# Second layer's weights decoded from copies shifted by 16 bits, and sums of low parts from the fourth tile on

## Chip, cores and metric

The kernel runs on one core of one Trainium2 chip. The metric is device time in microseconds of one execution, median of three runs. TensorE (PE), VectorE (DVE), ScalarE (ACT), GpSimd (POOL) and SyncE (SP) each work through their own queue in order and meet at semaphores.

## What is computed

A causal depthwise convolution over the sequence (7 softmaxed taps per head) is followed by two feed-forward layers without bias, all in float32 precision:

```python
out = einsum('hk,bskhg->bshg', softmax(weight), windows(x))   # x: (4, 4096, 192)
x = out.reshape(16384, 192)
h = x @ moe_w_in;  r = maximum(h, 0);  x = (r * r) @ moe_w_out       # 192 -> 2048 -> 192
h = x @ moe2_w_in; g = maximum(0.01 * h, h); out = g @ moe2_w_out
```

The four weight matrices arrive as float64 and are seen by the kernel as pairs of 32-bit words (low word, high word).

## The kernel before

**Precision.** PE multiplies in a float32 format with a shortened mantissa (`F32R`). Every operand is therefore split into a high part and a low part, and a product is made of high by high, high by low and low by high.

**Tiles and steps.** The 16384 tokens are 32 tiles of 512. A step is one pair p (0 to 7) of 128-wide chunks of the 2048 hidden columns, for one tile and one layer. Steps 0 to 15 take tiles 0 and 1 of layer 1 together; steps 16 to 23 are tile 2 of layer 1, 24 to 31 tile 3 of layer 1, 32 to 39 tile 0 of layer 2, and so on, 512 in all. In step s PE does the first product (`g1`) of step s+1, and the second product (`g2` or `g2_one`) of step s-2 (`LAG = 2`). PE works in two halves of 64 rows side by side, so that matmuls come in pairs; `g1` has 9 pairs. `g2_one` has 10 pairs as long as the low parts of the two chunks are multiplied apart, and 9 once a third operand, the sum of both low parts (`add_low`, tile `both`, written by DVE), and differences of weight blocks (`differences`, on POOL) let one product stand for two. Which of the two is used is `trick = s >= THREE`, with `THREE = 32`.

**What ACT and DVE do in a step.** ACT takes both chunks out of PSUM (`act`), squares them in layer 1 (`square`) and rounds them to the high part (`high`); DVE subtracts to get the low part (`low`), and adds where `trick` holds (`add_low`). The convolution of later tiles (`prep`), the splitting of results for the next layer (`leave`) and the decoding of weights (`dec`) are fitted between these by a planner (`fill` in `single`) with modelled costs; in steps 0 to 15 the order is written out by hand (`ROW`, one letter an operation: `L` a load of weights, `d` the next item of `dec`).

**Turns on a PSUM bank.** The two halves of PE take turns on the same accumulating bank. Where a bank goes from one half to the other, the order is kept by an empty instruction on POOL's queue that PE waits for:

```python
if holder.get((u, k), half) != half:
    done = nc.gpsimd.nop(nofuse=True).ins
    tc.add_manual_dep(done, lastly[u, k].name, in_turn, reason="halves take turns on a bank")
    tc.add_manual_dep(ins, done.name, in_turn, reason="halves take turns on a bank")
```

There is one of these in each paired step (L670) and three in each single step (L718). Nothing else on POOL is busy for long; its queue also issues a few DMAs (casts and integer adds) and runs `differences`.

**Decoding a weight.** The weights of one pair p of one layer are 768 pairs of words on each of 128 partitions, loaded by five DMAs on SP (`load`, `load_w`). For layer 2 DVE does: `mantissa` (L234) and `rest` (L250), which make the bits under the float32 mantissa from the low word; `exponent` (L266), after which ACT corrects the exponent (L269); `sign` (L281), followed by four DMAs on SP that put the high part in its places (L287); `power` (L296) and `low_` (L302, three pieces). Layer-2 pairs are decoded one after the other in about steps 13 to 38. The raw words of a pair lie in the memory that later holds the finished weights of another pair of layer 2 (`lent`, tags `w20` to `w27`), or in the staging tiles `y` and `w`.

Of the kernel before, what the change touches and what calls it, by code (L numbers as in the profile page):

```python
# [9 lines left out]
F32 = mybir.dt.float32  # L10
F32R = mybir.dt.float32r
I32 = mybir.dt.int32
U32 = mybir.dt.uint32
ACTF = mybir.ActivationFunctionType
ALU = mybir.AluOpType
# [3 lines left out]
P = 128  # L19
TT = 512  # L20
# [5 lines left out]
LAG = 2  # L26
AHEAD = 2
GAP = 5
SECOND, THIRD = 16, 36
THREE = 32  # L30
COVER = 2
# [7 lines left out]
CAST = ((1, 2), (1, 3))  # L39
ASIDE = (2, 3, 4)  # L40

# [13 lines left out]
    "ybpdwLAyBdpawThrp",  # L55
    "ldppABabhlp",
    "AyBydpabhdww",
    "lyAdappLhlBdwp",
    "pAbpayhBrbywd",
# [7 lines left out]
def conv_moe_moe2_kernel(  # L67
# [10 lines left out]
    nc = tc.nc  # L78
# [82 lines left out]
    def load_w(l, p, t):  # L161
# [10 lines left out]
        nc.sync.dma_start(out=to[:, :, 0:2 * R], in_=src[:, :, 2 * P:])  # L172

    held, holding = deque(), [False]
    ready, owner_m, raised_at, signed = {}, {}, {}, {}
# [24 lines left out]
    def decode(l, p, t, a, b):  # L200
# [22 lines left out]
        T = {}  # L223
        by_add = l == 1 and p >= ADD

        def mantissa():
# [27 lines left out]
        def exponent():  # L254
            release()
            if l == 1 and p > 0:
                if "t" not in words:
                    words["t"] = lent(0)
                T["t"] = words["t"][:, p % 2 * NW:(p % 2 + 1) * NW]
            elif l == 2 and p in ASIDE:  # L260
                if "t2" not in words:
                    words["t2"] = stage.tile([P, NW, 2], I32, tag="y", name="t2").rearrange("p n w -> p (n w)")
                T["t"] = words["t2"][:, p % 2 * NW:(p % 2 + 1) * NW]
# [28 lines left out]
        def power():  # L292
            if not (l == 1 and p > 0):
                owner_m["m"] = 0
            T["p"] = stage.tile([P, NW], I32, tag="t" if l == 1 and p > 0 else "m", name="p")[:, 0:n]
            nc.vector.tensor_scalar(out=T["p"], in0=T["t"], scalar1=-(2 ** 23), scalar2=None, op0=ALU.bitwise_and)  # L296

        def low_():
            assert not by_add or "added" in T
            ready[l, p, 1] = True  # L300
            for of, to in lows:
                nc.vector.scalar_tensor_tensor(  # L302
                    out=to, in0=of(T["r"]) if by_add else f32(of(lo_w)), scalar=2.0 ** -20, in1=f32(of(T["p"])), op0=ALU.mult, op1=ALU.mult
                )

        return [(one, mantissa), (two, rest)], [(one, exponent)], [(two, sign), (one, power), (two, low_)]


# [532 lines left out]
    def evac(u):  # L841
# [11 lines left out]
        def shift(i):  # L853
            if i == 0:
                z["s"], z["r"] = f32(stage.tile([P, NW], I32, tag="m", name="zs")[:, 0:TT]), ring[:, 2, :]
            nc.scalar.copy(out=z["s"][halves(i)], in_=o[i, "r"][halves(1 - i)])
# [27 lines left out]
    with tc.manual_schedule():  # L884
# [7 lines left out]
        def load(n):  # L892
# [3 lines left out]
            since[n] = now[0]  # L896
            if n < NP or NP + 1 < n < 2 * NP - 1:
                t = lent(n if n < NP else n + 1 - NP).rearrange("p (c w) -> p c w", w=2)
            else:
                t = stage.tile([P, NW, 2], I32, tag="w" if n == NP + 1 else "y", name="w")  # L900
            load_w(l, p, t)
            words[n] = t

        def fill_dec():
# [8 lines left out]
            def stage_(j, k):  # L913
                if j >= len(parts):
                    return
                n, a, b = parts[j]
                cost = {0: (780, 1180), 1: (620,), 2: (1230, 580, 1260)}
                l, p = loads[n]
                need = first_use["w", l, p] - LEAD_W - (((2 if p >= ADD else 3), 1, 0) if l == 1 else (4, 2, 1))[k]
                for m, c in enumerate(cost[k]):  # L920
                    def run(j=j, k=k, m=m, n=n):
                        if j not in got:
                            begin(j)
                        got[j][k][m][1]()
                    run.second = (k, m) in ((0, 1), (2, 2))
# [3 lines left out]
                    if l == 2 and k == 1 and p:  # L929
                        at_ = p - 2 if p in ASIDE[1:] else ASIDE[0] - 1 if p == ASIDE[-1] + 1 else p - 1  # L930
                        gate = lambda at_=at_: (p == ASIDE[0] or signed[2, at_] + 5000 <= clock["D"]) and not (
                            SECOND <= now[0] < THIRD and now[0] % NP == NP - 1
                        )
                    dec.append((need + (LATE and l == 1 and p >= ADD and (k, m) == (2, 2)) + (l == 2 and k == 2 and m > 0), c, run, gate))
                if k == 2 and a == 0:
                    if n in AFTER:
                        dec.append((need, 0, lambda n=n: load(AFTER[n]), None))

            stage_(0, 1)
            stage_(0, 0)  # L940
            for j in range(len(parts)):
                if parts[j][0] == NP - 1 or j == 0:
                    stage_(j, 2)
                    stage_(j + 1, 0)
                    stage_(j + 1, 1)
                else:
                    stage_(j + 1, 0)
                    early = j + 1 < len(parts) and parts[j + 1][0] - NP in ASIDE + (ASIDE[-1] + 1,)
                    if early:
                        stage_(j + 1, 1)  # L950
                    stage_(j, 2)
                    if not early:
                        stage_(j + 1, 1)
            for k in range(len(dec) - 2, -1, -1):
# [224 lines left out]
        def single(s, begun, u2, A, Z, leaving, then, alone):  # L1179
# [26 lines left out]
            do = {  # L1206
                "actA": lambda: act(*A), "actZ": lambda: act(*Z), "sqZ": lambda: square(*Z, trick), "sqA": lambda: square(*A, False),
                "hiA": lambda: high(*A), "hiZ": lambda: high(*Z), "loA": lambda: low(*A), "loZ": lambda: low(*Z),
# [33 lines left out]
        for s in range(NS):  # L1242
# [63 lines left out]
            begun += length(s - 1)  # L1306
            if s == 2 * NP:
                clock["D"] = clock["A"] = begun + 2500
            if late:
# [49 lines left out]
```

## Time and profile before

| | |
|---|---|
| median of 3 runs | 2041.4 us (2041.13 to 2041.49) |
| the profiled execution: own time, span | 2040.87 us, 2039.2 us |
| PE, PE weight load busy | 2030.6 us (100%), 1964.9 us (96%) |
| DVE, ACT, POOL busy | 1698.7 us (83%), 1458.2 us (72%), 42.2 us (2%) |
| granted TensorE clock | 1.00 in every stretch asked for |

The span is the stretch that the profiler covers; 1.67 us of the execution lie around it. Starts are in microseconds from the span's start. Step 17, the last paired one, has its second product at 96.1 to 98.7 us; step 26 starts at about 133, step 34 at about 166.

### The profile page before, as it was taken

To read this page: it belongs to the slowest core of one execution; us is meant where nothing else is said; L and a number is where in the kernel's file an instruction comes from. 1 tells how busy PE (TensorE), PEld (TensorE's weight loads), DVE (VectorE), ACT (ScalarE), POOL (GpSimd) and SP (SyncE) were. 2 spreads that over 40 slices of the span, in tenths; PEclk is the share of its full clock that TensorE was granted. 3 is DMA by queue.
4 is the path that set the end of the run, shared out by engine and by line. 5 is a ranking of instruction groups with operands and counts; after the bars stand their busy time and mean duration, and the time that the engine had idled before them with its cause. 6 is when DMAs were issued, how large, how long until landed. Compare 5 with 4: busy or idle time off the path is not lost.

```text
span 2039.2 us, 47094 instructions
## 1 busy us (share of the span) xinstructions
PE 2030.6 (100%) x18552; PEld 1964.9 (96%) x18552; DVE 1698.7 (83%) x2656; ACT 1458.2 (72%) x2638; POOL 42.2 (2%) x82
## 2 busy tenths in 40 slices
PE   9999999999999999999999999999999999999998
PEld 5999999999999999999999999999999999999998
DVE  8899878788887978879788897888878888798775
ACT  7897567676676866767677676766767667687675
POOL 1004010000000000000000000000000000000000
PEclk9999999999999999999999999999999999999999
DMA  8662121222212212131211212122122221221111
GB/s 189 146 160 75 25 45 27 49 30 49 38 27 52 37 44 36 30 60 30 48 26 39 52 27 48 29 50 38 27 49 30 49 38 27 52 35 42 24 30 27
DMA packets 240087, 98.66 MB, mean 48 GB/s; under 512 B 208568, under 2 KB 225080, under 8 KB 239864
## 3 DMA queue, kind: packets, MB, share of 16 engines
q1 hardware_dynamic: 236696, 92.54, 22.7%
q0 software_dynamic: 1168, 2.75, 0.7%
q8 instruction: 145, 2.38, 0.5%
q14 instruction: 78, 0.64, 0.1%
q10 hardware_dynamic: 2000, 0.36, 0.1%
HBM read 25.19 MB, written 12.58 MB: 19 GB/s over the span
## 4 chain that ended last, share of the span: by engine, by line
PE 98%; ACT 1%; DVE 0%; DMA 0%; issue 0%; POOL 0%; DVEq 0%; ACTq 0%; POOLq 0%
PE h L556 48%; PE o1m L556 16%; PE o1r L556 16%; PE o0m L556 8%; PE o0r L556 8%; PE conv L460 1%; PE idle_o L1003 0%; ACT g L588 0%; DMA w<-lent 0%; ACT g L597 0%; ACT hi L615 0%; DVE lo L619 0%; DVE w L302 0%; ACT x L487 0%; ACT ring L241 0%
## 5 line engine op out<-in xcount | busy, mean ns | idle before, releaser
L556 PE MATMUL h<-x,w 64*128 64x512 f32 x9216 | 1350.9, 376 | 0.5 <-DMA w<-lent 0.4
L556 PEld LDWEIGHTS h<-x,w 64*128 64x128 f32 x9216 | 1061.5, 186 | 7.3 <-ACT hi L615 0.8
L619 DVE TENSOR_TENSOR lo<-g,hi 128x512 fp32r<-128x512 f32 x1022 | 665.6, 689 | 266.2 <-ACT hi L615 250.6
L556 PE MATMUL o1m<-hi,w 64*128 64x512 f32 x2044 | 613.8, 378 | 0.3 <-ACT ring L755 0.3
L615 ACT CAST hi<-g 128x512 fp32r<-128x512 f32 x1020 | 586.1, 621 | 22.9 <-DVE g L595 12.9
L556 PE MATMUL o1r<-hi,w 64*128 64x512 f32 x2012 | 601.0, 378 | 0.0
L590 ACT ACTIVATE g<-h 128x512 f32<-128x512 f32 x512 | 281.7, 596 | 308.3 <-PE h L556 308.3
L588 ACT ACTIVATE g<-h 128x512 f32<-128x512 f32 x512 | 282.8, 596 | 159.8 <-PE h L556 159.5
L556 PEld LDWEIGHTS o1m<-hi,w 64*128 64x128 f32 x2044 | 359.2, 186 | 20.8 <-ACT ring L755 0.7
L556 PE MATMUL o1r<-lo,w 64*128 64x512 f32 (+1 forms) x990 | 372.6, 376 | 0.0
L556 PEld LDWEIGHTS o1r<-hi,w 64*128 64x128 f32 x2012 | 352.9, 186 | 20.2 <-ACT ring L752 0.3
L556 PE MATMUL o1m<-both,w 64*128 64x512 f32 x958 | 360.6, 376 | 0.0
L631 DVE TENSOR_TENSOR both<-lo 128x512 fp32r<-128x512 f32 x479 | 331.6, 692 | 20.7
L556 PE MATMUL o0m<-hi,w 64*128 64x512 f32 x1056 | 314.8, 378 | 0.0
L556 PE MATMUL o0r<-hi,w 64*128 64x512 f32 x1020 | 307.5, 379 | 0.0
L556 PE MATMUL o0m<-lo,w 64*128 64x512 f32 x544 | 202.6, 377 | 0.0
L556 PE MATMUL o0r<-lo,w 64*128 64x512 f32 (+1 forms) x542 | 201.6, 376 | 0.0
L556 PEld LDWEIGHTS o0m<-hi,w 64*128 64x128 f32 x1056 | 186.6, 186 | 0.7
L597 ACT ACTIVATE g<-g 128x512 f32<-128x512 f32 x285 | 177.7, 632 | 7.4
L556 PEld LDWEIGHTS o1r<-lo,w 64*128 64x128 f32 (+1 forms) x990 | 182.6, 184 | 0.3
L556 PEld LDWEIGHTS o0r<-hi,w 64*128 64x128 f32 x1020 | 180.2, 186 | 1.1 <-POOLq L718 0.7
L556 PEld LDWEIGHTS o1m<-both,w 64*128 64x128 f32 x958 | 178.4, 186 | 0.5 <-DVE both L631 0.3
(129 smaller groups left out, 1288.0 us busy)
## 6 DMA issues: line engine op xcount, KB each, us to landing
x<-x SPq DMA_DIRECT2D x189, 256.0 KB
out_dram<-y SPq DMA_DIRECT2D x188, 64.0 KB
raw_a<-in_x_dram SPq DMA_DIRECT2D x127, 64.0 KB
raw_b<-in_x_dram SPq DMA_DIRECT2D x62, 64.0 KB
lent<-in_moe_w_out_dram SPq DMA_DIRECT2D x13, 256.0 KB
lent<-in_moe_w_in_dram SPq DMA_DIRECT2D x13, 192.0 KB
w<-t SPq DMA_DIRECT2D x8, 256.0 KB
lent<-in_moe_w_in_dram SPq DMA_DIRECT2D x13, 128.0 KB
```

Of the source, the lines that this page charges most:

```text
L460: nc.tensor.matmul(out=acc, lhsT=diag[k], rhs=src, start=(k == 0), stop=(k == K - 1))
L556: return nc.tensor.matmul(out=o.rearrange("p (b a) -> p b a", a=2), lhsT=w, rhs=z.rearrange("p (a b) -> p b a", a=2), start=begin, stop=end_,)
L588: nc.scalar.activation(out=g, in_=hps.pop((u, f)), func=ACTF.Relu)
L590: nc.scalar.activation(out=g, in_=hps.pop((u, f)), func=ACTF.Prelu, alpha=0.01)
L597: nc.scalar.activation(out=g, in_=g, func=ACTF.Square)
L615: nc.scalar.copy(out=a, in_=gsp[u, f])
L619: nc.vector.tensor_sub(out=b, in0=gsp.pop((u, f)), in1=f32(hi[u, f]))
L631: nc.vector.tensor_add(out=c, in0=f32(lo[u, 2 * p]), in1=f32(lo[u, 2 * p + 1]))
```

## The change

Three things change together.

1. The bits under the mantissa of a layer-2 weight are no longer made by `mantissa` and `rest`. A DMA on POOL's queue (`shift`) copies the raw words of a pair by two bytes further, so that the wanted bits come to lie in one word, and DVE only masks them (`mask`); the scale of `low_` changes from 2^-20 to 2^-36. The eight copies go to `w27`, `w26`, `y`, `w27`, `y` and three times to the place of the pair's own finished weights. They are items of `dec` of cost 0: copies 0 and 1 behind the last item of layer 1, copies 2 and 3 behind the last item of pair 0 (and behind the load of pair 3, which is issued right there), copy 4 behind `mask` of pair 2, copies 5 to 7 behind the last item of the pair before. `mask` is let in by the planner when `SHIFTED` (6500 ns) have gone by its clock since the copy, and the copy's own time starts `LOADED` (6000 ns) after its load.
2. `THREE` is 24 and not 32: the sums of low parts begin with tile 3 of layer 1, and `differences` of layer 1 run in steps 18 to 25 and not 60 to 67. The square of the second chunk stays on ACT until step 36, as before.
3. The load of layer-2 pair 1 moves from row 13 to row 11 and goes to `w22` instead of tag `w`; the order of exponents in `dec` changes; exponents are stored in `t` and `m` in turn; `power` overwrites the raw high words; the planner's times of gates are shifted when its clock is set at step 16.

```diff
-THREE = 32
+THREE = 24
-ASIDE = (2, 3, 4)
+MOVED = ("w27", "w26", "y", "w27", "y", "own", "own", "own")
+SHIFTED, LOADED = 6500, 6000
...
-    "ldppABabhlp",
+    "LldppABabhlp",
     "AyBydpabhdww",
-    "lyAdappLhlBdwp",
+    "lyAdapphlBdwp",
...
+    def shift(p):
+        t, how = words[NP + p], MOVED[p]
+        if how in "wy":
+            z = stage.tile([P, NW, 2], I32, tag=how, name="shifted")
+        else:
+            z = const.tile([P, WIDE], I32, tag=f"w2{p}" if how == "own" else how, name="shifted")[:, 0:2 * NW]
+            z = z.rearrange("p (c w) -> p c w", w=2)
+        flat = lambda y: y.rearrange("p c w -> p (c w)").bitcast(I16)
+        nc.gpsimd.dma_start(out=flat(z)[:, 0:4 * NW - 1], in_=flat(t)[:, 1:4 * NW])
+        shifted[p] = z
+        shifted_at[p] = max(clock["D"], clock["A"], loaded_at[p])
...
+        moved = l == 2 and p < len(MOVED)
+        def mask():
+            T["r"] = t[:, a:b, 0]
+            nc.vector.tensor_scalar(out=T["r"], in0=shifted[p][:, :, 0], scalar1=2 ** 25 - 1, scalar2=None, op0=ALU.bitwise_and)
...
-        return [(one, mantissa), (two, rest)], [(one, exponent)], [(two, sign), (one, power), (two, low_)]
+        return [(one, mask)] if moved else [(one, mantissa), (two, rest)], [(one, exponent)], [(two, sign), (one, power), (two, low_)]
...
+                    if moved and k == 0:
+                        gate = lambda p=p: shifted_at[p] + SHIFTED <= clock["D"]
...
+                if moved and k == 0 and p == 2:
+                    dec.append((need, 0, lambda: shift(4), None))
                 if k == 2 and a == 0:
                     if n in AFTER:
                         dec.append((need, 0, lambda n=n: load(AFTER[n]), None))
+                    if n == NP - 1:
+                        dec.append((need, 0, lambda: (shift(0), shift(1)), None))
+                    if n == NP:
+                        dec.append((need, 0, lambda: (shift(2), shift(3)), None))
+                    if l == 2 and MOVED[p + 1:p + 2] == ("own",):
+                        dec.append((need, 0, lambda p=p: shift(p + 1), None))
...
-                chain += [("sqZ", *(("D", "sqZ") if trick else ("A", "sqA")), ("actZ",)), ("sqA", "A", "sqA", ())]
+                chain += [("sqZ", *(("D", "sqZ") if s >= THIRD else ("A", "sqA")), ("actZ",)), ("sqA", "A", "sqA", ())]
...
-            if first_use[1, 4] - 4 <= s < first_use[1, 4] - 4 + NP:
-                differences(1, s + 4 - first_use[1, 4])
+            if 2 * NP + LAG <= s < 3 * NP + LAG:
+                differences(1, s - 2 * NP - LAG)
```

## Rows read from the trace of the kernel before

**Rows 1.** The page: span, busy time of the engines, chain that ended last.
```profile
span 2039.2 us, 47094 instructions
PE 2030.6 (100%) x18552; PEld 1964.9 (96%) x18552; DVE 1698.7 (83%) x2656; ACT 1458.2 (72%) x2638; POOL 42.2 (2%) x82
PE 98%; ACT 1%; DVE 0%; DMA 0%; issue 0%; POOL 0%; DVEq 0%; ACTq 0%; POOLq 0%
```

**Rows 2.** Timeline of PE: start, length, instructions, count; single steps, before and after step 34.
```profile
148.26 1.75 PE L556 MATMUL h<-x,w 64*128 64x512 f32 x14
...
152.38 1.75 PE L556 MATMUL h<-x,w 64*128 64x512 f32 x14
...
185.13 1.32 PE L556 MATMUL h<-x,w 64*128 64x512 f32 x10
...
189.01 1.32 PE L556 MATMUL h<-x,w 64*128 64x512 f32 x10
```

**Rows 3.** Busy time in stretches: PE, PEld, DVE, ACT, POOL, clock, DMA share, GB/s.
```profile
96.50:100.50 4.00, 4.00 (x41) 3.78 (x38) 1.56 (x4) 1.97 (x4) 0.00 (x0) 1.00 0.01 2
...
133.00:137.10 4.10, 3.83 (x34) 3.24 (x34) 3.52 (x7) 3.81 (x8) 0.00 (x0) 1.00 0.85 205
137.10:141.20 4.10, 4.10 (x41) 4.09 (x39) 4.07 (x7) 4.07 (x8) 0.00 (x0) 1.00 0.45 123
```

**Rows 4.** Groups by line, 60 to 185 us.
```profile
L250 DVE SCALAR_TENSOR_TENSOR lent<-lent,m 128x768 f32<-128x768 uint32 x5 | 6.3, 1270 | 0.1
...
L631 DVE TENSOR_TENSOR both<-lo 128x512 fp32r<-128x512 f32 x5 | 3.5, 691 | 0.1
...
L234 DVE TENSOR_SCALAR m<-lent 128x768 int32<-128x768 int32 x5 | 3.6, 720 | 0.1
```

**Rows 5.** Timeline of POOL; in brackets its idle time before and what ended it.
```profile
34.22 1.30 POOL L245 DMA_DIRECT2D ring<-lent  x1 [21.80 <-ACT ring L241]
...
93.94 0.52 POOL L487 DMA_DIRECT2D x<-acc_b  x1 [24.24 <-PE o1r L556]
156.32 2.44 POOL L149 CAST w<-w 128x64 fp32r<-128x64 f32 x1 [61.86 <-PE o1r L556]
...
169.26 0.23 POOL L149 CAST w<-w 128x64 fp32r<-128x64 f32 x1
```

**Rows 6.** POOL's empty instructions (turns): steps 2, 16, 17 and 21.
```profile
L670 POOLq EVENT_SEMAPHORE  x1: 17/17/17, 34.5 to 34.5; - x1
L670 POOLq EVENT_SEMAPHORE  x1: 17/17/17, 93.3 to 93.3; - x1
L670 POOLq EVENT_SEMAPHORE  x1: 17/17/17, 97.4 to 97.4; - x1
L718 POOLq EVENT_SEMAPHORE  x3: 17/17/17, 112.7 to 113.5; - x3
```

**Rows 7.** Timeline of DVE, paired steps' end.
```profile
90.41 0.72 DVE L234 TENSOR_SCALAR m<-w 128x768 int32<-128x768 int32 x1 [0.78 <-DMA w<-in_moe_w_out_dram]
...
92.24 1.21 DVE L250 SCALAR_TENSOR_TENSOR w<-w,m 128x768 f32<-128x768 uint32 x1
```

**Rows 8.** Timeline of SP: loads of layer-2 pair 1, copies of the high part.
```profile
82.95 0.63 SPq L166 DMA_DIRECT2D w<-in_moe_w_in_dram  x1
...
85.72 0.47 SPq L172 DMA_DIRECT2D w<-in_moe_w_out_dram  x1
102.38 3.18 SPq L287 DMA_DIRECT2D w<-t  x4
```

**Rows 9.** DMA issues: count, KB each, median us from issue to landing.
```profile
ring<-m POOLq DMA_DIRECT2D x2, 384.0 KB, 5.5
...
x<-acc_b POOLq DMA_DIRECT2D x2, 128.0 KB, 2.7
```

**Rows 10.** Waits of PE: for whom, total us, times, longest; whole span, then 60 to 400 us.
```profile
PEld o0r L556 <- POOLq L718: 0.7, 4, 0.2
...
PEld o1m L556 <- ACT ring L755: 0.7, 1, 0.7
```

More of the change, by code (lines that the diff above doesn't have):

```diff
@@ L11 @@
 F32R = mybir.dt.float32r
+I16 = mybir.dt.int16
 I32 = mybir.dt.int32
@@ L172, in load_w @@
         nc.sync.dma_start(out=to[:, :, 0:2 * R], in_=src[:, :, 2 * P:])
+    shifted, shifted_at, loaded_at = {}, {}, {}
+    def shift(p):
[9 more added lines that the diff above has]
+        shifted_at[p] = max(clock["D"], clock["A"], loaded_at[p])
     held, holding = deque(), [False]
@@ L259, in exponent @@
                 T["t"] = words["t"][:, p % 2 * NW:(p % 2 + 1) * NW]
[L260 to L263, printed above, removed]
+            elif moved:
+                T["t"] = stage.tile([P, NW], I32, tag="tm"[p % 2], name="t")[:, 0:n]
             else:
@@ L294, in power @@
                 owner_m["m"] = 0
-            T["p"] = stage.tile([P, NW], I32, tag="t" if l == 1 and p > 0 else "m", name="p")[:, 0:n]
+            if moved:
+                T["p"] = t[:, a:b, 1]
+            else:
+                T["p"] = stage.tile([P, NW], I32, tag="t" if l == 1 and p > 0 else "m", name="p")[:, 0:n]
             nc.vector.tensor_scalar(out=T["p"], in0=T["t"], scalar1=-(2 ** 23), scalar2=None, op0=ALU.bitwise_and)
@@ L302, in low_ @@
                 nc.vector.scalar_tensor_tensor(
-                    out=to, in0=of(T["r"]) if by_add else f32(of(lo_w)), scalar=2.0 ** -20, in1=f32(of(T["p"])), op0=ALU.mult, op1=ALU.mult
+                    out=to, in0=of(T["r"]) if by_add or moved else f32(of(lo_w)), scalar=2.0 ** (-36 if moved else -20),
+                    in1=f32(of(T["p"])), op0=ALU.mult, op1=ALU.mult
                 )
-        return [(one, mantissa), (two, rest)], [(one, exponent)], [(two, sign), (one, power), (two, low_)]
+        return [(one, mask)] if moved else [(one, mantissa), (two, rest)], [(one, exponent)], [(two, sign), (one, power), (two, low_)]
     phases = [[(1, 0), (1, 1)], [(1, 2)], [(1, 3)], [(2, 0)], [(2, 1)], [(2, 2)], [(2, 3)]]
@@ L854, in shift @@
             if i == 0:
-                z["s"], z["r"] = f32(stage.tile([P, NW], I32, tag="m", name="zs")[:, 0:TT]), ring[:, 2, :]
+                z["s"], z["r"] = f32(stage.tile([P, NW, 2], I32, tag="w", name="zs").rearrange("p n w -> p (n w)")[:, 0:TT]), ring[:, 2, :]
             nc.scalar.copy(out=z["s"][halves(i)], in_=o[i, "r"][halves(1 - i)])
@@ L896, in load @@
             since[n] = now[0]
-            if n < NP or NP + 1 < n < 2 * NP - 1:
+            if n < NP or NP < n < 2 * NP - 1:
                 t = lent(n if n < NP else n + 1 - NP).rearrange("p (c w) -> p c w", w=2)
             else:
-                t = stage.tile([P, NW, 2], I32, tag="w" if n == NP + 1 else "y", name="w")
+                t = stage.tile([P, NW, 2], I32, tag="y", name="w")
             load_w(l, p, t)
             words[n] = t
+            loaded_at[n - NP] = max(clock["D"], clock["A"]) + LOADED
         def fill_dec():
@@ L916, in stage_ @@
                 n, a, b = parts[j]
-                cost = {0: (780, 1180), 1: (620,), 2: (1230, 580, 1260)}
                 l, p = loads[n]
+                moved = l == 2 and p < len(MOVED)
+                cost = {0: (620,) if moved else (780, 1180), 1: (620,), 2: (1230, 580, 1260)}
                 need = first_use["w", l, p] - LEAD_W - (((2 if p >= ADD else 3), 1, 0) if l == 1 else (4, 2, 1))[k]
@@ L924, in run @@
                         got[j][k][m][1]()
-                    run.second = (k, m) in ((0, 1), (2, 2))
+                    run.second = (k, m) in ((0, 1), (2, 2)) and not moved
                     gate = (lambda n=n: now[0] >= since[n] + 2) if k == 0 and m == 0 else None
@@ L941, in fill_dec @@
             for j in range(len(parts)):
-                if parts[j][0] == NP - 1 or j == 0:
+                n = parts[j][0]
+                if n == NP - 1:
+                    stage_(j, 2)
+                    stage_(j + 1, 1)
+                    stage_(j + 1, 0)
+                elif j == 0:
                     stage_(j, 2)
@@ L945, in fill_dec @@
                     stage_(j + 1, 1)
+                elif n < NP:
+                    stage_(j + 1, 0)
+                    stage_(j, 2)
+                    stage_(j + 1, 1)
+                elif n - NP + 1 < len(MOVED):
+                    stage_(j + 1, 1)
+                    stage_(j, 2)
+                    stage_(j + 1, 0)
                 else:
+                    stage_(j, 2)
                     stage_(j + 1, 0)
[L948 to L953, printed above, removed]
+                    stage_(j + 1, 1)
             for k in range(len(dec) - 2, -1, -1):
@@ L1307, in conv_moe_moe2_kernel @@
             if s == 2 * NP:
+                for at_ in (raised_at, signed, shifted_at, loaded_at):
+                    at_.update({k: min(z - max(clock.values()), 0) + begun + 2500 for k, z in at_.items()})
                 clock["D"] = clock["A"] = begun + 2500
```

8 lines of the change are left out of this document (4 added, 4 removed).

## The prediction

> **What bounds the kernel now.** I read the page first: PE is busy for the whole span and is 98% of the chain that ended last [rows 1], so a matmul that goes away is time gained, and time in which PE stands still is time lost, one for one. Then the timeline of PE for the length of a step: 152.38 - 148.26 = 4.12 us with 19 pairs of matmuls, 189.01 - 185.13 = 3.88 us with 18 [rows 2]; a pair is 4.12 / 19 = 0.216 us. Then the stretches around the change. At steps 26 and 27 DVE and ACT are nearly full beside PE (DVE 3.52, ACT 3.81 of the 4.10 us from 133.00) [rows 3], so they have little room, but they are not what PE waits for: PE's waits in the steady part are fractions of a microsecond, the longest 0.7 us for ACT's copy out of a bank at step 26 [rows 10]. Last I read POOL's queue, which looks empty (42.2 us busy) [rows 1] but carries the turns that PE waits for: one at 93.3 (step 16), one at 97.4 (step 17), three from 112.7 on (step 21) [rows 6]. So far PE has lost 0.7 us to them in all, in four waits [rows 10]. The reader is to see that a queue with no work can still be on PE's path.
>
> **Sums from step 24 on.** Steps 24 to 31 feed the second products of steps 26 to 33: eight steps with one pair less, 8 x 0.216 = 1.7 us off PE. It costs DVE 8 x 0.69 = 5.5 us of additions [rows 4]. The squares stay where they were. `differences` of layer 1 move into steps 18 to 25; they wait for nothing that comes later than PE's own order, and turns have passed beside such work before (see the waits of 0.7 us in all [rows 10]). I take nothing for them; the bound is 0 to 0.5 us.
>
> **Mask instead of mantissa and rest.** Per layer-2 pair DVE drops 0.72 + 1.27 us and does one mask, which I price like the mantissa's and-operation, 0.72 us [rows 4]: 8 x 1.27 = 10.2 us less DVE work, against the 5.5 us more. DVE ends 4.7 us lighter, but in stretches where PE does not wait for DVE. So this gives PE nothing, or at most the wait at step 26 (0.7 us) should ACT's order change for the better [rows 10]; bounds 0 to -0.8 us, I take 0.
>
> **The copies: what is queued behind them.** A copy is a DMA on POOL's queue, and that queue is kept in order. Two rows show it: the cast at 93.94 and the one at 156.32 are put down to a wait for PE [rows 5], and the first comes 0.6 us behind the turn at 93.3 [rows 6], which waits for PE. The issue itself is no trouble: 1.30 us from 34.22, with a turn at 34.5 inside it [rows 5, 6]. What counts is an issue that has to wait, for then the next turns stand behind it, and PE behind them.
>
> *Copies 0 and 1* (row 13) find their words loaded, since the load of pair 1 now starts two rows earlier; POOL takes them right behind the turn of step 13, four microseconds ahead of the next. Nothing. The load that moved up goes ahead of the high parts of layer 1's last pair on SP's queue; I give that 0 to 1 us and take 0.
>
> *Copies 2 and 3* stand in `dec` right behind the load of pair 3, and copy 3 reads what that load brings. Counting the letters `d` in `ROW` (47) and the 13 items decoded ahead, 60 items are taken by step 15; in the new order the sixtieth is `sign` of pair 0, so power and low part of pair 0, the load of pair 3 and copies 2 and 3 are taken in step 16, where the planner lets both pieces in (its DVE clock has 2.7 us free before the first low part). On POOL this is behind the turn of step 16 (93.3) and ahead of that of step 17 (97.4) [rows 6]. When does the load land? `sign` takes the place of the `rest` that starts at 92.24 [rows 7] and ends at about 93.4; its four copies of the high part occupy SP for 2.5 us (3.18 us at 102.38 [rows 8]), so the load starts at 95.9. The load of pair 1 started at 82.95 [rows 8] and DVE got its last piece at 90.41 [rows 7], 7.5 us later, on busy DMA queues; its five issues alone take 2.8 us (82.95 to 85.72 [rows 8]) and the smallest DMA with a known landing 2.7 us [rows 9], so 5.5 us is the light end. DMA is idle there (share 0.01 [rows 3]) and I take 5.5: landed at 101.4, turn at 101.7, against 97.4. PE stands for 4.3 us in step 17; bounds 2.8 us (`sign` 1.5 us earlier) and 6.3 us (7.5 us for the load).
>
> *Copy 4* stands behind `mask` of pair 2, which follows the load of pair 4 in `dec`; copy 4 reads that load. By the planner's costs the load falls in step 19 and the copy in step 20. On SP the load starts behind the copies of tile 0's operands, about 113.5 to 115.5 with everything 4.3 us late, and lands 5.5 us later at 119 to 121; the turn of step 21 would be due at 112.7 + 4.3 = 117.0 [rows 6]. 2 to 4 us; I take 2.5, bounds 0 and 5.
>
> *Copies 5, 6 and 7* go into memory that the pair before frees with its `low_`, so POOL waits for DVE's last piece in the same step. DVE's pieces of step s run about when PE is in step s+1, some before its first turn and some 0 to 1.8 us behind it. Three times 0 to 1.8; I take 0.5 each, 1.5 us together, bounds 0 and 5.
>
> **Sum.** -1.7 + 4.3 + 2.5 + 1.5 = +6.6 us. Made against the profiled execution's own time, 2040.87 us (span 2039.2 and 1.67 around it), that is 2047.5 us. The median of the runs shown is 0.5 us above that execution, so the median forecast is 2048.0 us, 0.32% slower.
>
> **A rule on slow issues.** POOL's work stretches beside DVE: the same cast took 2.44 us at 156.32 and 0.23 us at 169.26, 2.2 us more [rows 5]. The Trainium skill, page "SBUF — State Buffer", section "SBUF: two separate sides", says that a DMA issued by GpSimd has its descriptors written through a port that certain DVE instructions lock, so that one of 620 ns took about 3100 ns beside such an instruction. Estimated by that page each copy would come 2.5 us later, 8 x 2.5 = 20 us if all of it reached PE. The issue of 1.30 us at 34.22 speaks against the rule's size, the stretched cast for it [rows 5]; no copy of this size is in the trace.
>
> **Rivals.**
> *A, not slower:* POOL's waits end before the next turn is due. For copy 3 the load would have to land by 97.1, 1.2 us after I have it start; that needs `sign` some 4 us earlier or the load on SP ahead of the four copies. It decides at that one point: landing before 97.4 in step 17. Against it is the order of SP and of `dec`. For it: no long stall behind a turn is in the trace [rows 10]. Time: 2041.4 - 1.7 = 2039.7 us. A part of it (only copy 3 stalls PE, at its lower bound: -1.7 + 2.8) gives 2042.5 us.
> *B, copies late:* the copies' own landing is the new wait. 384 KB took 5.5 us [rows 9], and a copy has 768 KB; the planner allows 6.5. If issues stretch by the 2.2 us of the cast, the four copies whose masks follow at 6.5 us (0, 5, 6, 7) hold DVE up for 4 x 2.2 = 8.8 us; of that the 4.7 us that DVE is lighter are covered, and 4.1 us come on top of the forecast: 2052 us.
> *C, sums without effect:* the one pair less is lost because ACT, at 3.81 of 4.10 us in step 26 [rows 3], can't follow steps of 3.88 us. Then the 1.7 us are not gained: 2049.7 us.
>
> **Chances and range.** Forecast (PE stalls behind waiting copies, 5 us or more over the gain) 0.50, A in full 0.19, in part 0.15, B 0.10, C 0.06. 0.2% of 2041.4 is 4.1 us, about what a measurement of this kernel can tell from no change. Above 2045.5 lie B, C and most of the forecast (0.44 of 0.50): 0.60. Below 2037.3 would need A with all of PE's waits gone besides: 0.03. The rest, 0.37, is the same. The likeliest's own range is 2044 to 2052 us (bounds of the stalls: -1.7 + 2.8 + 0 + 1.5 to about +10.6). The range reaches down to A, 2039.4, and up to B, 2052.0.
>
> **What would show it.** In the timeline of POOL, a DMA of `shift` in step 16 whose idle time ends with the landing of the load of pair 3, and the turn of step 17 right behind it, near 101.7 and not 97.4; PE with a gap of some 4 us there, put down to POOL or its queue; a second gap near 117 to 121; `both` first at about 132 plus the stalls; steps 26 to 33 at 3.88 us. If PE runs through step 17 without a gap, the forecast is wrong at copies 2 and 3, and A holds. If gaps in DVE end with a landing of `shifted`, B holds.

## The result, and the profile after

The changed kernel takes 2069.1 us (median of four runs, 2068.0 to 2070.3) against 2041.3 us for the kernel before on the same chip (2040.9 to 2041.5): 27.8 us more, ratio 1.0137 with a 95% interval of 1.0119 to 1.0154. It is slower, as forecast, and by far more than the forecast of 2048.0 us; the time lies above the range of 2039.4 to 2052.0.

The page has the same bound as in [rows 1] and 28.8 us more of span. Its fourth line here is the queue of POOL's DMAs, with packets, MB and share:

```profile
span 2068.0 us, 47080 instructions
PE 2038.1 (99%) x18536; PEld 1963.1 (95%) x18536; DVE 1695.0 (82%) x2656; ACT 1458.1 (71%) x2638; POOL 48.2 (2%) x90
PE 93%; DVE 2%; DMA 2%; issue 1%; ACT 1%; SPq 1%; POOL 0%; POOLq 0%; DVEq 0%; ACTq 0%
...
q0 software_dynamic: 2320, 9.04, 1.5%
```

PE's busy time and POOL's 48 us say next to nothing; the chain that ended last has 93% of PE in it, where it had 98%. I call a time in which PE stands still a stand. The waits of PE over the whole span (for whom, total, times, longest), where [rows 10] had 0.7 us in four waits:

```profile
PE o1m L580 <- POOLq L742: 7.0, 1, 7.0
PE o0m L580 <- POOLq L694: 5.9, 1, 5.9
PE o1r L580 <- POOLq L742: 2.9, 3, 1.2
PE o0m L580 <- DVE lo L643: 2.6, 1, 2.6
```

POOL's timeline shows what the turns stood behind (copies 2, 3, 4 and 7; in brackets POOL's idle time and what ended it), against the turns of [rows 6]:

```profile
96.77 0.53 POOL L187 DMA_DIRECT2D shifted<-lent  x1 [13.17 <-DMA w<-t]
104.51 0.53 POOL L187 DMA_DIRECT2D shifted<-lent  x1 [7.21 <-DMA lent<-in_moe_w_out_dram]
...
126.20 0.58 POOL L187 DMA_DIRECT2D shifted<-lent  x1 [8.87 <-DMA lent<-in_moe_w_out_dram]
...
195.10 0.58 POOL L187 DMA_DIRECT2D shifted<-w  x1 [3.38 <-DVE w L325]
```

The turns themselves, by line and window: steps 16 and 17 and then the first two of step 20 in the changed kernel, and last the three of step 20 in the kernel before:

```profile
L694 POOLq EVENT_SEMAPHORE  x2: 17/17/17, 94.7 to 105.0; - x2
...
L742 POOLq EVENT_SEMAPHORE  x2: 17/17/17, 126.2 to 126.3; - x2
...
L718 POOLq EVENT_SEMAPHORE  x3: 17/17/17, 109.0 to 109.9; - x3
```

SP's timeline has the loads that copies 3 and 4 waited for, first issue of each:

```profile
96.00 0.66 SPq L168 DMA_DIRECT2D lent<-in_moe_w_in_dram  x1
...
119.10 0.80 SPq L168 DMA_DIRECT2D lent<-in_moe_w_in_dram  x1
```

And PE's timeline the two stands that follow, and a third at the end of layer 2's decode:

```profile
98.50 0.65 PE L580 MATMUL h<-x,w 64*128 64x512 f32 x4
105.06 0.79 PE L580 MATMUL o0m<-hi,w 64*128 64x512 f32 x1 [5.91 <-POOLq L694]
105.06 0.79 PE L580 MATMUL o1m<-hi,w 64*128 64x512 f32 x1
105.65 0.63 PE L580 MATMUL o0m<-hi,w 64*128 64x512 f32 x1
...
106.08 0.63 PE L580 MATMUL o0m<-lo,w 64*128 64x512 f32 x1
...
126.25 0.79 PE L580 MATMUL o1m<-hi,w 64*128 64x512 f32 x1 [7.00 <-POOLq L742]
...
165.47 1.29 PE L580 MATMUL h<-x,w 64*128 64x512 f32 x10
...
169.35 1.29 PE L580 MATMUL h<-x,w 64*128 64x512 f32 x10
...
201.28 0.45 PE L580 MATMUL o0m<-lo,w 64*128 64x512 f32 x1 [2.62 <-DVE lo L643]
```

Copy 3 is issued 8.5 us behind the first issue of its load (104.51 - 96.00), copy 4 7.1 us (126.20 - 119.10), and in the same half microsecond the turn passes (the turn of step 17 at 105.0) and PE goes on. From 98.50 four matmuls of 0.108 us should have been followed at once: 6.1 us are lost; before 126.25 it is 7.2 us. Behind each stand the pairs of matmuls are 0.43 us apart (105.65 to 106.08) and not 0.216. The stretches (columns as in [rows 3]) show why:

```profile
100.00:105.00 5.00, 0.00 (x0) 0.00 (x0) 0.00 (x0) 0.00 (x0) 0.49 (x1) 0.87 0.66 170
105.00:110.00 5.00, 4.94 (x24) 3.81 (x26) 2.41 (x4) 2.93 (x6) 0.56 (x2) 0.50 0.53 183
...
178.00:183.00 5.00, 4.07 (x39) 3.48 (x37) 4.08 (x8) 4.33 (x9) 4.55 (x7) 1.00 0.39 132
```

Behind the 6.1 us stand the granted clock is 0.50, the 1.2 GHz level, until about 110.9: half of 5.8 us, 2.9 us, is lost there. Behind 7.2 us at 126.25 it is 0.50 until about 131.4 (2.6 us), and behind the stand of 2.9 us at 201.28 it is 0.53 on the mean from 202.5 to 205.8 (1.6 us). Behind the 1.2 us stand at copy 6, inside 178 to 183, it stays 1.00.

The sum of PE's gaps, each read off PE's timeline to about 0.1 us: copies 2 and 3 9.0 us (6.1 + 2.9), copy 4 9.8 (7.2 + 2.6), copies 5 to 7 3.6 (0.9 + 1.2 + 1.5), the stand at 201 5.0 (2.9 + 0.5 behind it + 1.6; DVE's low part comes late there, behind the mask of pair 7), three waits for operands, sums and a bank 3.1 (1.2 + 1.2 + 0.7), together 30.5; less the 1.7 us of shorter steps (169.35 - 165.47 = 3.88 us from step 26 on) 28.8, beside 28.8 us of span.

### The profile page after: what moved, and what is told of

Read it like the earlier page. It is cut to its first block, busy times and chain, and to the rows that moved or that the text cites. A ratio compares the mean times of both kernels' runs of the same rounds, so it can differ in the third digit from the quotient of the medians.

```text
span 2068.0 us, 47080 instructions
## 1 busy us (share of the span) xinstructions
PE 2038.1 (99%) x18536; PEld 1963.1 (95%) x18536; DVE 1695.0 (82%) x2656; ACT 1458.1 (71%) x2638; POOL 48.2 (2%) x90
## 4 chain that ended last, share of the span: by engine, by line
PE 93%; DVE 2%; DMA 2%; issue 1%; ACT 1%; SPq 1%; POOL 0%; POOLq 0%; DVEq 0%; ACTq 0%
PE h L580 46%; PE o1m L580 16%; PE o1r L580 16%; PE o0m L580 8%; PE o0r L580 8%; DMA lent<-in_moe_w_out_dram 1%; DVE lo L643 0%; ACT g L621 0%; ACT g L612 0%; DMA w<-lent 0%; DMA shifted<-w 0%; DVE t L301 0%; DVE acc_b L471 0%; ACT hi L639 0%; DMA shifted<-lent 0%
## 5 line engine op out<-in xcount | busy, mean ns | idle before, releaser
L643 DVE TENSOR_TENSOR lo<-g,hi 128x512 fp32r<-128x512 f32 x1022 | 664.4, 688 | 285.6 <-ACT hi L639 271.4
L580 PE MATMUL o1r<-lo,w 64*128 64x512 f32 (+1 forms) x1006 | 379.1, 377 | 0.0
L580 PE MATMUL o1m<-both,w 64*128 64x512 f32 x974 | 366.9, 377 | 1.1 <-DVE both L655 1.1
L655 DVE TENSOR_TENSOR both<-lo 128x512 fp32r<-128x512 f32 x487 | 337.0, 692 | 21.1
```

The lines of the kernel that those rows point to most:

```text
L580: return nc.tensor.matmul(out=o.rearrange("p (b a) -> p b a", a=2), lhsT=w, rhs=z.rearrange("p (a b) -> p b a", a=2), start=begin, stop=end_,)
L643: nc.vector.tensor_sub(out=b, in0=gsp.pop((u, f)), in1=f32(hi[u, f]))
L655: nc.vector.tensor_add(out=c, in0=f32(lo[u, 2 * p]), in1=f32(lo[u, 2 * p + 1]))
```

## Experiments

Each time stands beside the kernel before on the same chip, 2040.4 to 2041.1 us.

### POOL's queue

**All copies on SP's queue**, nothing else changed:

```diff
-        nc.gpsimd.dma_start(out=flat(z)[:, 0:4 * NW - 1], in_=flat(t)[:, 1:4 * NW])
+        nc.sync.dma_start(out=flat(z)[:, 0:4 * NW - 1], in_=flat(t)[:, 1:4 * NW])
```

> The changed kernel with the eight shifted copies issued on SP's queue and not on POOL's; same copies, same order, same bytes. Theory (turns stand behind waiting copies): the gaps of PE put down to POOL's queue go, those at about 99 and 119 us first, and with them the falls of the granted clock; what stays is DVE's wait for the last copies and the late operand copy, 2042 to 2047 us, no stretch at clock 0.50. Rival (traffic of the copies, or DVE waiting for them, holds PE up): above 2060 us with gaps at the same places.

Measured: 2053.3 us, ratio 1.0060 (1.0046 to 1.0073). The cost falls from 27.8 to 12.3 us, so 15.5 us hang on the queue that issues the copies and 12.3 us do not. The time lies between the two expectations, and the clock still falls, against the theory: it is 0.50 from 185 to 190 us. No wait of PE for POOL's queue is left among the long ones; DVE's low parts have their place:

```profile
PE o0m L580 <- DVE lo L643: 4.4, 3, 3.3
PE o1m L580 <- DVE lo L643: 4.2, 3, 3.4
```

What DVE stood for, in its timeline (an exponent, L286, behind the copying of earlier high parts; a mask, L246, behind a copy):

```profile
128.90 0.56 DVE L286 TENSOR_SCALAR t<-lent 128x768 int32<-128x768 int32 x1 [4.30 <-DMA w<-t]
...
183.58 0.56 DVE L246 TENSOR_SCALAR w<-shifted 128x768 int32<-128x768 int32 x1 [3.55 <-DMA shifted<-w]
```

**A small waiting DMA in the kernel before**, 32 B on each partition, right behind the load of layer-2 pair 3 in `dec` (and one pair later, as control):

```diff
+        tiny = const.tile([P, 4, 2], I32, name="tiny")
...
+                    if n == NP:   # NP + 1 in the control
+                        dec.append((need, 0, lambda: nc.gpsimd.dma_start(out=tiny, in_=words[NP + 3][:, 0:4]), None))
```

> The kernel before with one small DMA added on POOL's queue, 32 bytes per partition from the words of layer-2 pair 3 to a tile that nothing reads, right behind the load of these words; no shifted copies. Theory: the wait alone stops PE: the turn of the next step stands until the load has landed, 6 to 9 us, and the granted clock falls to 0.50 for a stretch behind it, 3 to 4 us more: 2050 to 2054 us. Rival (it takes the 768 KB of the copies): within 1 us of before.

> The kernel before with the same small DMA on POOL's queue that cost 10.1 us behind a load still under way, now a pair of decode later, when the load has long landed. Theory (the wait is what costs, not the DMA): 2040 to 2042.5 us, no wait of PE for POOL's queue above 1.5 us. Rival (any DMA on that queue, or the DMA's own issue, holds the turns up): 2045 us or more.

Measured: 2051.1 us, 10.1 us slower, ratio 1.0050 (1.0035 to 1.0066); one pair later 2041.3 us, ratio 1.0002 (0.9993 to 1.0011). The same DMA is free when its data is there. In the first, the waits of PE, POOL's timeline and a stretch:

```profile
PE o1r L556 <- POOLq L718: 7.4, 1, 7.4
```
```profile
113.16 0.58 POOL L940 DMA_DIRECT2D tiny<-lent  x1 [17.80 <-DMA lent<-in_moe_w_out_dram]
```
```profile
110.00:115.00 5.00, 1.79 (x8) 1.52 (x10) 0.97 (x2) 0.00 (x0) 0.58 (x1) 0.50 0.58 176
```

A stand of 7.4 us costs 10.1 us, and the clock is at 0.50 behind it. By the Trainium skill, page "DMA: Bandwidth & Descriptors", section "Anatomy of one DMA — SWDGE (gpsimd) path", a DMA's wait is kept by the sequencer that issues it, ahead of the dispatch, and not by the DMA engines. By that rule the size of the DMA doesn't matter, and the traces agree: PE stands 7.4 us behind the waiting DMA of 4 KB, and 6.1 and 7.2 us behind those of 768 KB.

**Single copies taken off POOL's queue** in the changed kernel, with `p in (2, 3)`, then `(4,)`, `(5, 6, 7)` and `(2, 3, 4)`:

```diff
-        nc.gpsimd.dma_start(out=flat(z)[:, 0:4 * NW - 1], in_=flat(t)[:, 1:4 * NW])
+        (nc.sync if p in (2, 3) else nc.gpsimd).dma_start(out=flat(z)[:, 0:4 * NW - 1], in_=flat(t)[:, 1:4 * NW])
```

> The changed kernel (2069.1 us) with copies 2 and 3 alone on SP's queue, the others on POOL's. Theory (this pair costs what PE's gap shows: 6.1 us of stand and 3.6 us of slow clock behind it): 9 to 11 us less, 2058 to 2060.5 us. Rival (the stand is only made up later, or SP's wait delays the next load): 2063 us or more.

> The changed kernel with copy 4 alone on SP's queue. Theory (it costs 7.2 us of stand and 3.4 us of slow clock): 9 to 11 us less, 2058 to 2060.5 us. Rival (given back behind it, as DVE's exponents and masks then come late): 2063 us or more.

> The changed kernel with copies 5, 6 and 7 alone on SP's queue. Theory (POOL's waits for DVE's last piece cost the 0.9, 1.2 and 1.5 us that PE's gaps show there): 3 to 4.5 us less, 2064.5 to 2066.5 us. Rival (masks are late either way, and DVE takes POOL's place): 2068 to 2071 us.

> The changed kernel with copies 2, 3 and 4 on SP's queue: both long stands away. Theory (the two add): about 20 us less, 2048 to 2051 us. Rival (as with all eight on SP's queue, 2053.3 us, DVE's waits for copied high parts and masks take their place): 2053 to 2058 us.

| on SP's queue | us | less than 2069.1 | ratio to before (95%) |
|---|---|---|---|
| 2, 3 | 2060.8 | 8.3 | 1.0097 (1.0082 to 1.0112) |
| 4 | 2064.0 | 5.1 | 1.0109 (1.0094 to 1.0124) |
| 5, 6, 7 | 2067.7 | 1.4 | 1.0129 (1.0112 to 1.0146) |
| 2, 3, 4 | 2056.1 | 13.0 | 1.0074 (1.0059 to 1.0089) |

What comes back adds up, 8.3 + 5.1 = 13.4 beside 13.0, but it is less than the gaps (18.8 us for copies 2 to 4): the fourth run is the rival's, and so is the second. For copies 2 and 3 the theory is missed by little. Copy 4's gap is worth half, 5.1 us of 9.8, since DVE stands next and PE loses 3.6 us before 137.8. Copies 5 to 7, 1.4 us, lie between the two expectations. DVE's timeline with copy 4 alone moved:

```profile
136.60 0.56 DVE L286 TENSOR_SCALAR t<-lent 128x768 int32<-128x768 int32 x1 [4.29 <-DMA w<-t]
```

With copies 2 and 3 moved, SP's timeline also says how long that load takes by itself, first issue and copy 3 behind it:

```profile
95.84 0.66 SPq L168 DMA_DIRECT2D lent<-in_moe_w_in_dram  x1
...
101.65 0.50 SPq L187 DMA_DIRECT2D shifted<-lent  x1
```

5.8 us, where it was 8.5 us with copy 2 on POOL's queue. There copy 2 was issued at 96.77, in the middle of the load; here at 99.1, when all five parts of the load were issued. The difference comes back in other runs: copy 3 goes out 7.9 to 8.9 us behind the load's first issue in the four runs with copy 2 on POOL's queue inside the load (2064.0, 2067.7, 2069.1 and 2070.1 us), 5.6 to 6.0 us in six of the seven with copy 2 behind the load on SP's queue, and 7.1 us in the seventh (2056.1 us).

**Copies 3 and 4 one pair later in `dec`**, and then **copies 2, 3 and 4 held until 9 us of planned time behind the start of their load**, all on POOL's queue:

```diff
-                if moved and k == 0 and p == 2:
-                    dec.append((need, 0, lambda: shift(4), None))
...
-                        dec.append((need, 0, lambda: (shift(2), shift(3)), None))
+                        dec.append((need, 0, lambda: shift(2), None))
+                    if n in (NP + 1, NP + 2):
+                        dec.append((need, 0, lambda p=p: shift(p + 2), None))
```
```diff
-                    dec.append((need, 0, lambda: shift(4), None))
+                    dec.append((need, 0, lambda: shift(4), lambda: loaded_at[4] + 3000 <= clock["D"]))
...
-                        dec.append((need, 0, lambda: (shift(2), shift(3)), None))
+                        dec.append((need, 0, lambda: (shift(2), shift(3)), lambda: loaded_at[3] + 3000 <= clock["D"]))
```

> The changed kernel with copies 3 and 4 one pair later in the order of decoding, so that the load that each reads has landed; still on POOL's queue. Theory: the two longest gaps of PE, 6.1 and 7.2 us, and the slow matmuls behind them, 3.6 and 3.4 us, go: about 20 us less, 2049 us; the gaps at copies 5 to 7 stay. Rival (a copy on POOL's queue holds PE whatever it waits for): little change, above 2060 us.

> The changed kernel, copies still on POOL's queue, but copies 2, 3 and 4 are put into the order only 9 us of planned time behind the start of their load, so that POOL should not stand. Theory (PE stands because the copies wait for loads under way, not because there are copies): the two stands of 6 and 7 us with the slow clock behind them go, 18 to 20 us less, 2049 to 2053 us. Rival (what is late is the masks and the high parts; DVE stands in place of POOL): 2056 us or more.

Measured: 2056.2 us, ratio 1.0077 (1.0063 to 1.0090), and 2063.0 us, ratio 1.0110 (1.0094 to 1.0127). The first lies between theory and rival: behind copy 3 PE does not stand any more, but copy 4, now at 122.80, waits for DVE's mask (4.55 us of POOL's idle time end with it) and PE stands 3.3 us behind it. In the second PE has no gap over 0.4 us from 93 to 138 us, so the two stands do go, but 22 us are lost all the same: the later copies now hold up masks, PE waits for sums in their place (3.3 us at 171), and three waits for POOL's queue stay (1.8, 1.4 and 2.6 us). Theory right on the place, rival right on the time. DVE's timeline there:

```profile
168.57 0.56 DVE L246 TENSOR_SCALAR lent<-shifted 128x768 int32<-128x768 int32 x1 [6.30 <-DMA shifted<-lent]
...
178.18 0.56 DVE L246 TENSOR_SCALAR lent<-shifted 128x768 int32<-128x768 int32 x1 [3.99 <-DMA shifted<-lent]
```

### The sums

**The sums alone**, on the kernel before; and of these **the differences alone** (the last hunk):

```diff
-THREE = 32
+THREE = 24
...
-                chain += [("sqZ", *(("D", "sqZ") if trick else ("A", "sqA")), ("actZ",)), ("sqA", "A", "sqA", ())]
+                chain += [("sqZ", *(("D", "sqZ") if s >= THIRD else ("A", "sqA")), ("actZ",)), ("sqA", "A", "sqA", ())]
...
-            if first_use[1, 4] - 4 <= s < first_use[1, 4] - 4 + NP:
-                differences(1, s + 4 - first_use[1, 4])
+            if 2 * NP + LAG <= s < 3 * NP + LAG:
+                differences(1, s - 2 * NP - LAG)
```

> The kernel before with the sums of low parts and the differences moved to the fourth tile, weights decoded as before. Theory (all of the loss comes from copies that wait on POOL's queue): eight steps with one pair less, 8 x 0.216 = 1.7 us faster than before, 2039.6 us. Rival (the sums themselves cost, since DVE is nearly full in steps 24 to 31 and PE waits for both): same as before or slower, 2041 to 2045 us.

> The kernel before, with only the weight differences of layer 1 (POOL's work) made in steps 18 to 25; sums stay at step 32. Theory (the 11.7 us of the sums are DVE's additions): 2040 to 2042.5 us. Rival (the differences on POOL, or their wait, take part of it): 2044 to 2053 us.

Measured: 2052.7 us, 11.7 us slower, ratio 1.0056 (1.0043 to 1.0069), so that the gain of 1.7 us falls for the sums by themselves, and the rival's 2045 us are passed too; the differences alone 2040.7 us, ratio 0.9999 (0.9990 to 1.0008). With the sums alone PE's longest waits are for DVE's low parts, and DVE's timeline shows what is ahead of them:

```profile
PE o0m L556 <- DVE lo L619: 4.5, 2, 2.5
```

```profile
161.11 0.82 DVE L266 TENSOR_SCALAR t<-lent 128x768 int32<-128x768 int32 x1
161.81 1.23 DVE L281 SCALAR_TENSOR_TENSOR t<-lent,t 128x768 int32<-128x768 int32 x1
...
166.86 1.29 DVE L619 TENSOR_TENSOR lo<-g,hi 128x512 fp32r<-128x512 f32 x2
...
178.89 0.70 DVE L266 TENSOR_SCALAR t<-lent 128x768 int32<-128x768 int32 x1 [1.91 <-DMA w<-t]
```

With the additions in steps 24 to 31 the planner puts off decode until it is due, and then takes it in one go, 161.11 to 166.86, ahead of the low parts that PE stands for; the next exponent waits for high parts that were copied late.

**Is it DVE's load?** `rest` of layer 2 is left out, 10 us of DVE, with the sums alone and on the kernel before; the low parts of layer 2's weights are then made of the raw high words.

```diff
+            if l == 2:
+                return
             nc.vector.scalar_tensor_tensor(
...
-                    out=to, in0=of(T["r"]) if by_add else f32(of(lo_w)), scalar=2.0 ** -20, in1=f32(of(T["p"])), op0=ALU.mult, op1=ALU.mult
+                    out=to, in0=of(T["r"]) if by_add else f32(of(hi_w if l == 2 else lo_w)), scalar=2.0 ** -20, in1=f32(of(T["p"])), op0=ALU.mult, op1=ALU.mult
...
-                cost = {0: (780, 1180), 1: (620,), 2: (1230, 580, 1260)}
+                cost = {0: (780, 40 if l == 2 else 1180), 1: (620,), 2: (1230, 580, 1260)}
```

> The sums alone (2052.7 us), with the operation called rest of all layer-2 pairs left out (1.27 us of DVE each, 10.2 us together; the planner counts 40 ns for it, and the low part of layer 2's weights is made from the raw high words, so the output is another). Theory (the sums' 5.5 us of additions crowd the decode on DVE, and 10 us less of decode make the room): 2039 to 2043 us. Rival (the sums cost by their place in the order, or by their own lateness, whatever DVE has to do): 2049 us or more.

> The kernel before with rest of all layer-2 pairs left out in the same way, sums at step 32: the control. Theory (DVE has room enough before, so 10 us less of its work give PE nothing): 2040 to 2042 us. Rival (DVE is on PE's path already): 2039 us or less.

Measured: 2043.6 us, ratio 1.0013 (1.0003 to 1.0023), just above the theory's 2039 to 2043, and 2041.1 us, ratio 1.0001 (0.9992 to 1.0010). Ten microseconds off DVE are worth nothing by themselves and 8.6 us where the sums crowd it: 11.7 us over the kernel before have become 3.1. The planner counts less for `rest` here and so orders the other work anew; the two are not told apart.

**The change without the sums** (`THREE = 32` again, copies on POOL's queue):

> The changed kernel with the sums back at step 32 (copies still on POOL's queue). The sums alone cost 11.7 us on the kernel before. Theory (two separate costs: DVE's additions, and PE behind waiting copies): the copies alone cost what is left of the 27.8 us, so 2055 to 2060 us, with PE gaps of some 6 and 7 us put down to POOL's queue at copies 2 to 4. Rival (the lighter decode pays for the additions, so beside the copies the sums are worth their 1.7 us after all): 2067 to 2071 us.

Measured: 2070.1 us, ratio 1.0139 (1.0124 to 1.0154). The theory of two separate costs falls: 11.7 and 29.2 us don't add to 27.8. In the changed kernel, beside the lighter decode, the sums take 1.4 us off, near their 1.7 but too little to be told from nothing by these intervals.

### What the new order of decode costs

Copies on SP's queue in all four: with the sums at step 32; the same with high parts in three buffers in turn; with sums at step 24 and exponents let in 9 us behind a sign and not 5; and with the first five pairs alone decoded from copies (gate 8 us).

```diff
-THREE = 24
+THREE = 32
```
```diff
-                T["t"] = stage.tile([P, NW], I32, tag="tm"[p % 2], name="t")[:, 0:n]
+                if p in (2, 5):
+                    T["t"] = stage.tile([P, NW, 2], I32, tag="w", name="t").rearrange("p n w -> p (n w)")[:, 0:n]
+                else:
+                    T["t"] = stage.tile([P, NW], I32, tag="tm"[p % 3], name="t")[:, 0:n]
...
-                    if l == 2 and k == 1 and p > 1:
-                        at_ = p - 2 if p < len(MOVED) else p - 1 if p > len(MOVED) else len(MOVED) - 2 + len(MOVED) % 2
+                    if l == 2 and k == 1 and p in (3, 4, 6, 7):
+                        at_ = p - 3 if p < len(MOVED) else p - 1 if p > len(MOVED) else len(MOVED) - 2 + len(MOVED) % 2
```
```diff
-                        gate = lambda at_=at_: signed[2, at_] + 5000 <= clock["D"] and not (
+                        gate = lambda at_=at_: signed[2, at_] + 9000 <= clock["D"] and not (
```
```diff
-MOVED = ("w27", "w26", "y", "w27", "y", "own", "own", "own")
+MOVED = ("w27", "w26", "y", "w27", "y")
```

> The changed kernel with its copies on SP's queue and the sums back at step 32: the new decode alone, with nothing behind POOL's queue. Theory (the copies cost by their queue, the sums by DVE's additions): 2040 to 2044 us. Rival (DVE waits for masks and for loads by the new order of the decode, with or without the sums): 2046 to 2053 us, PE put down to DVE's low parts in steps 24 to 48.

> Copies on SP's queue, sums at step 32, and the high parts in three buffers in turn (the tile of the sums serves as third until step 32), so that an exponent waits for high parts copied three pairs before and not two. With two buffers and all else the same it was 2048.6 us with one stand of PE of 5.0 us, of which DVE's exponent waited 5.6 us for that copy. Theory (that one wait, with the slow clock behind it, is what the new decode still costs): 2040 to 2043 us. Rival (another piece of DVE is late next): 2045 to 2049 us.

> Copies on SP's queue, sums at step 24 (2053.3 us with the gate of 5 us), and exponents let in 9 us behind the sign of two pairs before, not 5. Theory (DVE waits because the planner lets exponents in before the high parts are copied): the stand of 3.6 us at 126 goes, and 2045 to 2049 us are left, since the stand at 181 waits for a mask. Rival (the exponent is only forced in later, ahead of due low parts): 2052 us or more.

> Copies on SP's queue, only for the first five pairs of layer 2 (pairs 5 to 7 decoded as before), sums at step 24, gate of exponents 8 us. Theory (the late stands come from copies 5 to 7, which wait for memory of the pair before, and from the gate): 2041 to 2046 us. Rival (without the lighter decode in steps 36 to 48 the additions crowd DVE as with the sums alone): 2048 us or more.

Measured: 2048.6 us, ratio 1.0036 (1.0023 to 1.0048); 2047.9, 1.0033 (1.0021 to 1.0044); 2055.0, 1.0071 (1.0056 to 1.0086); 2050.1, 1.0043 (1.0028 to 1.0058). Each time lies in the rival's range. DVE's timeline of the first and of the second:

```profile
128.86 0.56 DVE L286 TENSOR_SCALAR t<-lent 128x768 int32<-128x768 int32 x1 [5.64 <-DMA w<-t]
```
```profile
132.82 0.56 DVE L289 TENSOR_SCALAR t<-lent 128x768 int32<-128x768 int32 x1 [5.20 <-DMA lent<-in_moe_w_out_dram]
```

In the first an exponent stands 5.6 us for a buffer; with a third buffer one stands 5.2 us for its load. With the gate of 9 us PE has no gap at 126 any more, and masks are late in its place: PE loses 5.3 us before 173.0 and 4.1 us before 188.5. In each pair load, copy, mask, high parts and the next load follow one another through one queue of SP, and a link made faster shows the next. None of these beats the kernel before. The first of the four also tells what the sums cost: it differs from the run with all copies on SP's queue by the sums alone, and the two stand 7.8 and 12.3 us over the kernel before. So the sums cost 4.5 us there, with the lighter decode in place; the two intervals hardly touch.

## Why the prediction came out as it did

**Right: the place.** Copies 2 and 3 are issued in step 16, the idle time of POOL ends with the landing of a load, the turn of step 17 stands behind it, and PE with it; a second stand is at copy 4. The load of pair 3 starts at 96.0, as worked out (95.9). That a queue with nothing to do can bind PE is shown by the 32-byte DMA.

**Wrong: the sizes.** For the copies the mechanism held; the terms for the stands were too small, and two costs had no term. The stands behind POOL's queue, 8.3 us in the forecast (4.3 + 2.5 + 1.5), measured 16.9 (6.1 + 7.2 + 3.6); the slow clock behind the two long ones came to 5.5, and stands for DVE, an operand and a bank, with the clock behind one of them, to 8.1 (5.0 + 3.1). Even with each term at its upper bound the prediction's sum would have been 2056 us (-1.7 + 6.3 + 5 + 5 over 2041.4), and its range stopped at 2052.

The terms, in the order of the sum:

*Copies 2 and 3, 4.3 us.* The step "DMA is idle there (share 0.01) and I take 5.5": the load by itself does take about that (5.8 us with copy 2 behind it), but copy 2, which goes out 0.8 us behind the load's first issue, is itself 768 KB of traffic. It was 8.5 us to copy 3, above the 7.5 us of the bound. PE's gap, 6.1 us, is just within its bound of 6.3, as the turn was due later too (98.9 and not 97.4). Taking the pair off the queue gave back 8.3 us.

*Copy 4, 2.5 us.* The step "the copy in step 20" fails: the copy is taken one step earlier, and what stands behind it is the turn of step 20, at 109.0 in the kernel before, and not that of step 21 at 112.7. That is 3.7 us more to wait, and the load takes 7.1 us to the copy and not 5.5. That all is some 10 us late by then (1.2 for an operand and 9.0) and not 4.3 moves the load (119.10 and not 113.5 to 115.5) and the turn (due at 119.1) alike, and explains none of it. The gap was 7.2 us; 5.1 us come back when copy 4 is moved.

*What no term had: the clock.* A stand was counted once. After 6.1 and 7.2 us of it the granted clock was 0.50 for 5 to 6 us more, 2.9 and 2.6 us; the stand of 7.4 us made by the small DMA cost 10.1.

*Copies 5 to 7, 1.5 us.* The gaps are 3.6 us, moving them gave 1.4: right within its bounds of 0 to 5.

*The decode, 0 us.* The step "in stretches where PE does not wait for DVE. So this gives PE nothing" holds for what DVE does, as leaving out `rest` shows (1.0001). It does not hold for what DVE waits for: with neither POOL's queue nor sums in the way the new order still costs 7.8 us (2048.6), since an exponent that stands for a copy or a load holds the low parts behind it.

*The sums, -1.7 us.* In the whole change the times agree with the term (29.2 without, 27.8 with), but not for the reason given, and that is luck: on the old decode the same sums cost 11.7 us, so DVE's 5.5 us were not hidden there, and on the new decode with the copies on SP's queue they cost 4.5 us (12.3 and 7.8). So the mask paid for a part of them at most; why they cost nothing where PE also stands behind POOL's queue is not shown. The differences were free, as said.

**The rivals.** A is excluded. B is right in part: the masks of pairs 6 and 7 hold DVE up, as two rows of the changed kernel's DVE show,

```profile
184.37 0.75 DVE L246 TENSOR_SCALAR lent<-shifted 128x768 int32<-128x768 int32 x1 [2.22 <-DMA shifted<-lent]
...
199.37 0.56 DVE L246 TENSOR_SCALAR w<-shifted 128x768 int32<-128x768 int32 x1 [4.57 <-DMA shifted<-w]
```

but not by slow copies; behind the second PE stands at 201.28. Issued, they land sooner than the planner's 6.5 us; the DMA issues of the page (count, KB each, median us to landing):

```profile
shifted<-lent POOLq DMA_DIRECT2D x6, 767.8 KB, 4.4
```

Copy 7 was issued late, at 195.10, behind the last piece of the pair before. C is excluded: steps of 3.88 us are kept from step 26 on.

**The rule on slow issues.** The copies' issues took 0.53 to 0.58 us in all eight, also from 80 to 85 us with DVE busy for 4.52 of 5.00. The size given by the Trainium skill, page "SBUF — State Buffer", section "SBUF: two separate sides", 3100 ns and not 620, is not seen; but DVE was at tensor-tensor and scalar-tensor-tensor instructions (L643, L471) beside five of the issues and idle at three, so other instructions were not tried. The stretched cast speaks less for the rule than the prediction has it: beside the cast of 0.23 us DVE was busy as well, with a low part of 1.50 us from 169.26. By the Trainium skill, page "DMA: Bandwidth & Descriptors", section "Anatomy of one DMA — SWDGE (gpsimd) path", 2.0 us and the bytes at 436 GB/s, a copy would be an estimated 3.8 us (2.0 + 786,000 bytes / 436 GB/s); 4.4 us were measured.

**Open.** That copy 2 delays the load by its traffic, and not by something else that its earlier issue brings, is argued from the eleven runs and not shown apart; in one of them the load took 7.1 us without it. Whether a better order of the decode would gain the 1.7 us of the sums isn't shown; five versions on SP's queue did not.

## What to carry to other kernels

When a DMA goes onto a queue, ask first whether its data is there at that moment, then what stands behind it; its size and the queue's busy time say nothing about that. Price a stand of TensorE by its length and by the slow clock that the traces show behind stands of like length; between 2 and 4 us these traces show both levels, so take a price with and one without it. Count the change's own transfers as traffic beside the load that it waits for. Work that is hidden on a nearly full engine in one order may not be in another: try an edit that adds to it alone before its gain is counted, and look at what its queued pieces wait for, not only at how long they run.

## What the runs showed of the hardware

The granted clock was 0.50 behind stands of PE of 6.1 to 7.4 us (105 to 111 and 126 to 131 us in the changed kernel, 113 to 115 beside the small DMA), and 1.00 behind those of 0.9 to 1.5 us. In between the length alone does not decide: it was 0.50 behind a stand of 3.6 us (185 to 190 with all copies on SP's queue), 0.53 on the mean behind the one of 2.9 us and 0.50 behind one of 2.2 us (170.5 to 173.5 in the change without the sums), but 1.00 behind one of 3.3 us (122.8 to 128 with copies 3 and 4 one pair later). One load of 768 KB in five DMAs had landed 5.8 us behind its first issue, or 7.0 us with two operand copies of 256 KB behind it (106.15 to 113.16 beside the small DMA), or 8.5 us with a copy of 768 KB issued in its middle.
